# Unread products between the three pieces of the first expert's x, and narrowing steps of expert 0 shifted by one place

## The chip, the core and the metric

The kernel runs on one core of a Trainium2 chip. A core has TensorE (PE: matrix products, with PEld for its weight loads), VectorE (DVE), ScalarE (ACT), GpSimd (POOL) and SyncE (SP, which here only issues DMAs); each works through its own list of instructions in order and waits at an instruction until what that instruction reads has been written, or what it overwrites has been read. The metric is the device time of one execution in microseconds (us), as the median of several runs.

## The reference

Three layers stand one behind the other, all in float32:

```
state = alpha[t] * state + k[t] (x) v[t];  y[t] = q[t] @ state      # 4 x 8 heads, 768 steps, 48 wide
logits = x @ w_gate                                                  # x: 3072 tokens x 384
# greedy over all (token, expert) pairs by logit, each expert takes at most 384 tokens
out[mask_e] = relu(x[mask_e] @ w1[e]) @ w2[e]                        # 8 experts, 384 -> 1024 -> 384
h = out @ w_in;  result = (relu(h) ** 2) @ w_out                     # 384 -> 2048 -> 384
```

So every token goes through exactly one expert and then through a second, shared pair of matrices, w_in and w_out.

## The kernel before

**The stages.** The first 150 us are the attention (24 blocks of 128 steps). Then the experts follow one by one, and each is taken with the 384 tokens that are assigned to it: a router step finds the expert that fills first and its tokens, POOL gathers their rows of x from DRAM in three pieces of 128 tokens, PE transposes the pieces, and four chains of products follow: gemm1 (x by w1, 8 blocks f), gemm2 (by w2), gemm3 (by w_in, 16 blocks f) and gemm4 (by w_out). Each product in float32 accuracy is three products of rounded parts (high by high, low by high, high by low), so a block of gemm1, 2, 3 or 4 is nine products of 128x384. The expert that is done first is called expert 0 here, the next one expert 1.

**The first x.** For expert 0, `x_tr(0)` transposes piece after piece (j = 0, 1, 2; three transposes each) into PSUM, and `evac` copies to a rounded high part xh on ACT and the remainder xl on DVE: once for pieces 0 and 1 together, once for piece 2. Ahead of it the router writes the token numbers ix, and `warm(24)` puts 24 products on PE whose result (in acc[2]) nobody reads. `warm` is there from before at two other places too (3 and 8 products).

**The narrowing.** w_in and w_out come in as 64-bit words that hold float64 numbers, and `narrow` turns each of the 16 blocks of weights into a float32 number and splits that into a high and a low part. It is a generator with four steps for each block, which this text calls A (line 183), B (187), C (191) and D (203), all on DVE; each is two instructions of 128x384 while expert 0 runs. Between C and D, ACT must round the number to the high part (line 197, called H here, two instructions): it is put into `pend` at C and recorded at the next call of `highs()`, or at the latest in D. D subtracts the high part. H also overwrites the raw words, so it waits for C.

**Where the steps stand.** All order is the order in which the Python code records instructions, engine by engine. In gemm1 of expert 0, `highs(); next(wl[0], None); next(nw, None)` runs one narrowing step per block f, behind the splitting of one piece of the expert's own weights (lines 841 and 842). In gemm3 and gemm4 of expert 0 there are two steps per block f: one behind gemm3(f+1) and one behind gemm4(f), each behind a call of `highs()`. The steps are used up within block 12. gemm3(f) reads block f of the narrowed weights.

**What else stands on DVE there.** For each block gl (line 956), the low part of the squared activations, which the third product of gemm4 reads; two pieces of the next expert's weights (lines 813 on ACT and 814 on DVE); the router of expert 1, which runs in small steps between the products (counts on PE at line 464, votes at line 537, comparisons at line 456 on DVE), and the first part of the router of expert 2 (from line 426); and from block 12 on the evacuation of expert 1's x (`xl`, line 860), of which the next transposes (line 878) wait, since they use the same PSUM buffer xq_p.

Of the kernel before, what the change touches and what calls it, by code (L numbers as in the profile page):

```python
# [53 lines left out]
def kernel(ctx, tc, q, k, al, v, wg, w1, w2, w_in, w_out, out):  # L54
# [118 lines left out]
    def narrow():  # L173

        for f in range(NF2):
            raw = raws[f, 0]
            if fine[0] is None:
                ps = [(aw.tile([128, NWP], U32, name="nb"), slice(0, NWP))]
            else:
                ps = [(fine[0].tile([128, DM], U32, name="nb", tag="ob", bufs=3), slice(i * DM, (i + 1) * DM))  # L180
                      for i in range(2)]
            for t, cs in ps:
                nc.vector.tensor_scalar(t, raw[:, cs, 1], 3, 0x3FFFFFF8, op0=OP.logical_shift_left,
                                        op1=OP.bitwise_and)
            yield
            for t, cs in ps:
                nc.vector.scalar_tensor_tensor(t, raw[:, cs, 1], 0xC0000000, t, op0=OP.bitwise_and,
                                               op1=OP.bitwise_or)
            yield
            for t, cs in ps:  # L190
                nc.vector.scalar_tensor_tensor(t, raw[:, cs, 0], 29, t, op0=OP.logical_shift_right,  # L191
                                               op1=OP.bitwise_or)
            w = consts.tile([128, 2, NWP], FR, name=f"w{f}", tag=f"w{f}")

            def high(w=w, ps=ps):
                for t, cs in ps:
                    nc.scalar.activation(w[:, 0, cs], t.bitcast(FT), AF.Copy)

            pend.append(high)
            yield  # L200
            highs()
            for t, cs in ps:
                nc.vector.tensor_tensor(w[:, 1, cs], t.bitcast(FT), w[:, 0, cs].bitcast(FT), op=OP.subtract)  # L203
            wi[f] = w[:, :, :DM].rearrange("p h (a b) -> p h a b", a=KD)
            wo[f] = w[:, :, DM:]
            yield
# [3 lines left out]
    def highs():  # L210

        while pend:
            pend.pop()()
# [175 lines left out]
    def warm(n):  # L389

        jf = jc.rearrange("p a b -> p (a b)")
        for _ in range(n):
            nc.tensor.matmul(acc[2], jf[:, :128], jf[:, 128:128 + CAP], start=True, stop=True)
# [98 lines left out]
    def routing(kk):  # L492
# [155 lines left out]
            yield  # L648
            nc.tensor.matmul(fp, low, pr_, start=True, stop=True)
        if kk == 0:  # L650
            warm(24)
        ix = mr.tile([128, NT], I32, name="ix", bufs=2)
        for g in range(4):
            V.tensor_scalar(ix[32 * g:32 * (g + 1)], fp[:, NT * g:NT * (g + 1)], float(N // 2), None,
# [42 lines left out]
    nw = narrow()  # L697
# [149 lines left out]
    def w_upto(n):  # L847

        while wdone[0] < min(n, 24):
            next(wl[0])  # L850
            wdone[0] += 1

    def x_tr(kk):
        xh = mw.tile([128, KD, CAP], FR, name="xh", tag="tzh")
        xl = mw.tile([128, KD, CAP], FR, name="xl", tag="tzl")
        XT[kk] = (xh, xl)

        def evac(kd, xf, a=0, b=CAP):
            nc.scalar.activation(xh[:, kd, a:b], xf, AF.Copy)
            nc.vector.tensor_tensor(xl[:, kd, a:b], xf, xh[:, kd, a:b].bitcast(FT), op=OP.subtract)  # L860

        if kk == 0:
            banks = [xq_p, hu_p[0], hu_p[2]]
            banks = [[b[:, j * 128:(j + 1) * 128] for b in banks] for j in range(NT - 1)]
            banks.append([a[:, :128] for a in acc])
            for j in range(NT):
                for kd in range(KD):
                    nc.tensor.transpose(banks[j][kd], XG[kk][:, j, kd * 128:(kd + 1) * 128], ident)
                if j == NT - 2:
                    for kd, b in enumerate((xq_p, hu_p[0], hu_p[2])):  # L870
                        evac(kd, b[:, :256], 0, 256)
                elif j:
                    for kd in range(KD):
                        evac(kd, banks[j][kd], 256, CAP)
            return
        for kd in range(KD):
            for j in range(NT):
                nc.tensor.transpose(xq_p[:, j * 128:(j + 1) * 128], XG[kk][:, j, kd * 128:(kd + 1) * 128], ident)  # L878
            evac(kd, xq_p)
            yield  # L880
# [29 lines left out]
    def gemm1(kk, f):  # L910
        xh, xl = XT[kk]
        hp = hu()
        cs = slice(f % 2 * 128, (f % 2 + 1) * 128)
        for kd in range(KD):
            mm3(hp, (w1h[:, f // 2, kd, cs], w1l[:, f // 2, kd, cs]), (xh[:, kd, :], xl[:, kd, :]), kd == 0,
                kd == KD - 1)
            tick()
        hh = mw.tile([128, CAP], FR, name="hh", tag="eh")
        hl = mw.tile([128, CAP], FR, name="hl", tag="el")
        nc.scalar.activation(hh, hp, AF.Relu)  # L920
        nc.vector.scalar_tensor_tensor(hl, hp, 0.0, hh.bitcast(FT), op0=OP.max, op1=OP.subtract)  # L921
        return hh, hl

    def gemm2(f, h, ms=range(KD)):
        for m in ms:
            cs = slice(m * 128, (m + 1) * 128)
            mm3(acc[m], (w2h[:, f, cs], w2l[:, f, cs]), h, f == 0, f == NF1 - 1)
            tick()

    def z_evac():  # L930
        zh = mw.tile([128, KD, CAP], FR, name="zh", tag="tzh")
        zl = mw.tile([128, KD, CAP], FR, name="zl", tag="tzl")
        for m in range(KD):
            nc.scalar.activation(zh[:, m, :], acc[m], AF.Copy)
            nc.vector.tensor_tensor(zl[:, m, :], acc[m], zh[:, m, :].bitcast(FT), op=OP.subtract)
        return zh, zl
# [61 lines left out]
    def wstep():  # L998
        if wdelay[0] > 0:
            wdelay[0] -= 1  # L1000
        else:
            w_upto(wdone[0] + 1)
# [7 lines left out]
    for _ in x_tr(0):  # L1010
        pass
    h = gemm1(0, 0)
    rn = routing(1)
    for kk in range(E):
        more = kk + 1 < E
        rt[0] = rn if more else iter(())
        held[:] = True, False
        for f in range(NF1):
            if f == 0:
                beat[:] = (T0 if kk else 11), T1  # L1020
            if f == NF1 - 1:
                beat[0] = T2
            hn = gemm1(kk, f + 1) if f + 1 < NF1 else None
            if kk == 0:
                highs()
                next(wl[0], None)
                next(nw, None)
                if f == 0:
                    next(rn)
            w_upto(15 + 3 * (f // 2))  # L1030
            wstep()
            wstep()
            if f == NF1 - 2:
                gemm2(f, h, (0, 1))
                h6 = h
            elif f == NF1 - 1:
                gemm2(f, h, (0,))
                gemm2(f - 1, h6, (2,))
                gemm2(f, h, (1, 2))
            else:  # L1040
                gemm2(f, h)
            h = hn
        held[0] = False
        z = z_evac()
        g = gemm3(z, 0)
        beat[1] = T3
        for f in range(NF2):
            if not more and f == NF2 - 3:

                g1 = gemm3(z, f + 1)  # L1050
                g2 = gemm3(z, f + 2, True)
                for fj, gj, j in ((f, g, 0), (f + 1, g1, 0), (f, g, 1), (f + 1, g1, 1), (f + 2, g2, 0)):
                    gemm4(fj, gj, (j,))
                o_evac(kk, (0,))
                gemm4(f + 2, g2, (1,))
                o_evac(kk, (1,))
                for fj, gj in ((f, g), (f + 1, g1), (f + 2, g2)):
                    gemm4(fj, gj, (2,))
                o_evac(kk, (2,))
                return  # L1060
            if f + 1 < NF2:
                gn = gemm3(z, f + 1)
            elif more:
                for _ in rt[0]:
                    pass
                w_upto(12)
                h = gemm1(kk + 1, 0)
            if kk == 0:
                highs()
                next(nw, None)  # L1070
            if more and f == XF + 3:
                next(xt, None)
            gemm4(f, g)
            g = gn
            if kk == 0:
                highs()
                next(nw, None)
            wstep()
            if more and f == XF:
                for _ in rt[0]:  # L1080
                    pass
                xt = x_tr(kk + 1)
            if more and f > XF:
                next(xt, None)
            if kk + 2 < E and f == 11:
                rn = routing(kk + 2)
                next(rn)
            if kk + 2 < E and f == 13:
                next(rn)
        o_evac(kk)  # L1090
# [48 lines left out]
```

## Time and profile before

| what | value |
|---|---|
| runs without profile | 836.4, 837.15, 839.09 us; median 837.15 |
| the profiled execution's own time | 840.04 us, of which the span of the trace is 837.7 |
| PE busy | 778.7 us, 93% of the span |
| DVE busy | 532.7 us, 64% |
| ACT busy | 390.9 us, 47% |
| mean granted clock of PE | 0.968 of full speed |
| share of PE in the chain that ended last | 63% |

Times in the rows are microseconds from the start of the span. A granted clock of 1.00 is 2.4 GHz, 0.50 is 1.2 GHz. In a timeline the first number is the start, the second the duration, and the bracket at the end says how long the engine had been idle and what it had waited for. PE's products overlap: a stream of products of 128x384 starts one every 0.17 us at full clock although each lasts 0.33.

### The profile page before, as it was taken

Reading aid. Unit: us, or ns where it says so; the run is one execution under the profiler, and the core shown is the slowest. Engines: PE = TensorE matmul, PEld = TensorE weight load, DVE = VectorE, ACT = ScalarE, POOL = GpSimd, SP = SyncE. Lnnn points to the kernel's source line nnn. Section 1 sums busy time; section 2 is a strip of 40 time slices with the busy share of each in tenths; the row PEclk is TensorE's granted clock in tenths of the full one; section 3 lists DMA queues with packets and bytes.
Section 4 is the critical chain, followed back from the end, with each engine's and each line's share of the span. In section 5 each row is a group of like instructions: output and inputs, shape, how many; then the busy total and the mean of one; then the engine's idle time right before and its main releaser. Section 6 shows DMA issues by size and latency. Waiting matters only on the chain.

```text
span 837.7 us, 15297 instructions
## 1 busy us (share of the span) xinstructions
PE 778.7 (93%) x5830; PEld 733.1 (88%) x5830; DVE 532.7 (64%) x1454; ACT 390.9 (47%) x934; POOL 126.0 (15%) x146
## 2 busy tenths in 40 slices
PE   3888887788998899999999999999999999999996
PEld 2766666568997899999999999999999999999996
DVE  7999998757788665676567656665765543442211
ACT  2656655222455424643463456245524643661443
POOL 3222210020001211122112211221211110101001
PEclk9989999579999899999999999999999999999999
DMA  8998886150022100320131023004200330310000
GB/s 303 236 264 259 256 255 246 67 180 1 1 76 85 49 1 29 114 67 2 57 110 42 1 76 103 30 1 123 86 1 24 119 109 15 89 35 29 1 1 28
DMA packets 32440, 74.77 MB, mean 89 GB/s; under 512 B 4128, under 2 KB 14112, under 8 KB 32368
## 3 DMA queue, kind: packets, MB, share of 16 engines
q1 hardware_dynamic: 25840, 59.65, 23.7%
q0 software_dynamic: 3072, 9.44, 3.3%
q10 hardware_dynamic: 3456, 4.72, 1.6%
q8 instruction: 45, 0.74, 0.4%
q14 instruction: 27, 0.22, 0.1%
HBM read 64.36 MB, written 9.44 MB: 88 GB/s over the span
## 4 chain that ended last, share of the span: by engine, by line
PE 63%; issue 9%; DVE 6%; ACT 2%; POOL 1%; DMA 1%; SPq 0%; ACTq 0%; POOLq 0%; DVEq 0%
PE hu_p L885 10%; PE hu_p L887 10%; PE hu_p L886 10%; PE acc L969 7%; PE acc L965 6%; PE acc L970 6%; PE acc L885 3%; PE acc L887 3%; PE acc L886 3%; PE rt_p L464 1%; DVE nb L191 1%; PE xq_p L878 1%; PE rt_p L472 1%; POOL out_dram L991 1%; DVE w L203 1%
## 5 line engine op out<-in xcount | busy, mean ns | idle before, releaser
L956 DVE TENSOR_TENSOR gl<-rg,gh 128x384 fp32r<-128x384 f32 x127 | 72.0, 567 | 159.1 <-ACT rg L955 158.3
L953 ACT ACTIVATE rg<-hu_p 128x384 f32<-128x384 f32 x128 | 62.9, 491 | 157.6 <-PE hu_p L887 156.6
L885 PE MATMUL hu_p<-zh,w 128*128 128x384 f32 x384 | 132.9, 346 | 0.0
L969 PE MATMUL acc<-w,gh 128*128 128x384 f32 x381 | 130.6, 343 | 0.0
L887 PE MATMUL hu_p<-zl,w 128*128 128x384 f32 x384 | 130.1, 339 | 0.0
L886 PE MATMUL hu_p<-zh,w 128*128 128x384 f32 x384 | 130.1, 339 | 0.0
L965 PE MATMUL acc<-w,gl 128*128 128x384 f32 x381 | 126.4, 339 | 3.2 <-DVE gl L956 3.2
L970 PE MATMUL acc<-w,gh 128*128 128x384 f32 x381 | 128.0, 336 | 0.0
L920 ACT ACTIVATE hh<-hu_p 128x384 fp32r<-128x384 f32 x64 | 31.5, 492 | 148.8 <-PE hu_p L887 136.7
L921 DVE SCALAR_TENSOR_TENSOR hl<-hu_p,hh 128x384 fp32r<-128x384 f32 x64 | 35.6, 556 | 69.7 <-ACT hh L920 69.7
L484 POOL PARTITION_ALL_REDUCE tot<-ex x40 | 43.1, 1079 | 227.9 <-DVE ex L481 227.9
L965 PEld LDWEIGHTS acc<-w,gl 128*128 128x128 f32 x381 | 71.6, 189 | 4.5 <-DVE gl L956 4.4
L887 PEld LDWEIGHTS hu_p<-zl,w 128*128 128x128 f32 x384 | 72.4, 189 | 1.0
L885 PEld LDWEIGHTS hu_p<-zh,w 128*128 128x128 f32 x384 | 72.5, 189 | 0.1
L886 PEld LDWEIGHTS hu_p<-zh,w 128*128 128x128 f32 x384 | 72.6, 189 | 0.0
L969 PEld LDWEIGHTS acc<-w,gh 128*128 128x128 f32 x381 | 71.9, 189 | 0.6 <-ACT gh L954 0.4
L970 PEld LDWEIGHTS acc<-w,gh 128*128 128x128 f32 x381 | 71.9, 189 | 0.0
L954 ACT ACTIVATE gh<-rg 128x384 fp32r<-128x384 f32 x127 | 66.7, 525 | 4.0
L885 PE MATMUL hu_p<-xh,w1h 128*128 128x384 f32 x192 | 67.0, 349 | 0.0
L887 PE MATMUL hu_p<-xl,w1h 128*128 128x384 f32 x192 | 65.9, 343 | 0.0
L885 PE MATMUL acc<-hh,w2h 128*128 128x384 f32 x192 | 65.7, 342 | 0.0
L886 PE MATMUL hu_p<-xh,w1l 128*128 128x384 f32 x192 | 65.5, 341 | 0.0
(238 smaller groups left out, 1500.0 us busy)
## 6 DMA issues: line engine op xcount, KB each, us to landing
wraw<-in_w_dram SPq DMA_DIRECT2D x62, 384.0 KB, 3.2
raw<-in_w_in_dram SPq DMA_DIRECT2D x16, 384.0 KB, 6.3
raw<-in_w_out_dram SPq DMA_DIRECT2D x16, 384.0 KB, 7.9
vt<-in_v_dram SPq DMA_DIRECT2D x12, 384.0 KB, 6.9
x_d<-xo ACTq DMA_DIRECT2D x24, 192.0 KB, 4.6
a<-in_al_dram SPq DMA_DIRECT2D x9, 451.9 KB, 6.6
k<-in_k_dram SPq DMA_DIRECT2D x9, 448.0 KB, 6.2
q<-in_q_dram SPq DMA_DIRECT2D x9, 448.0 KB, 5.4
```

The costliest lines, as they stand in the source:

```text
L484: nc.gpsimd.partition_all_reduce(tot[:, :, :J], ex[:, :, :J], 128, bass_isa.ReduceOp.add)
L885: nc.tensor.matmul(dst, wh, xh, start=first, stop=False)
L886: nc.tensor.matmul(dst, wl, xh, start=False, stop=False)
L887: nc.tensor.matmul(dst, wh, xl, start=False, stop=last)
L920: nc.scalar.activation(hh, hp, AF.Relu)
L921: nc.vector.scalar_tensor_tensor(hl, hp, 0.0, hh.bitcast(FT), op0=OP.max, op1=OP.subtract)
L953: nc.scalar.activation(r, up, AF.Relu)
L954: nc.scalar.activation(gh, r, AF.Square)
L956: nc.vector.tensor_tensor(gl, g, gh.bitcast(FT), op=OP.subtract)
L965: nc.tensor.matmul(acc[j], gl[:, j * 128:(j + 1) * 128], wo[f][:, 0, :], start=False, stop=(f == NF2 - 1))
L969: nc.tensor.matmul(acc[j], gh[:, cs], wo[f][:, 0, :], start=(f == 0), stop=False)
L970: nc.tensor.matmul(acc[j], gh[:, cs], wo[f][:, 1, :], start=False, stop=False)
```

## The change

Three edits. In the router of expert 0, 29 unread products stand where 24 stood. In `x_tr(0)`, five unread products stand behind the transposes of piece 0 and three behind those of piece 1. And in gemm1 of expert 0, block f = 3 runs a second narrowing step, so that from there on every narrowing step of expert 0 stands one place earlier.

```
@@ routing, expert 0
-            warm(24)
+            warm(29)
@@ x_tr(0)
             for j in range(NT):
                 for kd in range(KD):
                     nc.tensor.transpose(banks[j][kd], XG[kk][:, j, kd * 128:(kd + 1) * 128], ident)
+                warm((5, 3, 0)[j])
                 if j == NT - 2:
@@ gemm1 of expert 0
                 next(nw, None)
                 if f == 0:
                     next(rn)
+                if f == 3:
+                    next(nw, None)
```

PE, between the transposes of piece 1 and those of piece 2 (xg is the gathered x, jc a table of constants); the rows with + are new.

```order
 L868 MATMUL xq_p<-ident,xg 128x128
 L868 MATMUL hu_p_2098<-ident,xg 128x128
 L868 MATMUL hu_p_2100<-ident,xg 128x128
+L393 LDWEIGHTS jc
+L393 MATMUL acc_2103<-jc 128x384
+L393 LDWEIGHTS jc
+L393 MATMUL acc_2103<-jc 128x384
+L393 LDWEIGHTS jc
+L393 MATMUL acc_2103<-jc 128x384
 L868 MATMUL acc_2101<-ident,xg 128x128
 L868 MATMUL acc_2102<-ident,xg 128x128
 L868 MATMUL acc_2103<-ident,xg 128x128
```

Three products more stand ahead of the transposes of the last piece; behind piece 0 five stand in the same way.

DVE, in gemm3 and gemm4 of expert 0, blocks 10 and 11 (gl as above; 814 splits the next expert's weights; 191 is C, 203 D, 183 A, 187 B). Before:

```order
L956 TENSOR_TENSOR gl<-rg,gh 128x384
L814 TENSOR_TENSOR w1l<-wraw,w1h 128x256
L191 SCALAR_TENSOR_TENSOR nb<-raw_1818,nb 128x384 x2
L203 TENSOR_TENSOR w_3191<-nb,w_3191 128x384 x2
L814 TENSOR_TENSOR w1l<-wraw,w1h 128x256
L956 TENSOR_TENSOR gl<-rg,gh 128x384
L814 TENSOR_TENSOR w2l<-wraw,w2h 128x256
L183 TENSOR_SCALAR nb<-raw_1821 128x384 x2
L187 SCALAR_TENSOR_TENSOR nb<-raw_1821,nb 128x384 x2
L814 TENSOR_TENSOR w2l<-wraw,w2h 128x256
```

The same two blocks after (gl is line 957 there):

```order
L957 TENSOR_TENSOR gl<-rg,gh 128x384
L814 TENSOR_TENSOR w1l<-wraw,w1h 128x256
L203 TENSOR_TENSOR w_3182<-nb,w_3182 128x384 x2
L183 TENSOR_SCALAR nb<-raw_1821 128x384 x2
L814 TENSOR_TENSOR w1l<-wraw,w1h 128x256
L957 TENSOR_TENSOR gl<-rg,gh 128x384
L814 TENSOR_TENSOR w2l<-wraw,w2h 128x256
L187 SCALAR_TENSOR_TENSOR nb<-raw_1821,nb 128x384 x2
L191 SCALAR_TENSOR_TENSOR nb<-raw_1821,nb 128x384 x2
L814 TENSOR_TENSOR w2l<-wraw,w2h 128x256
```

C and D stood side by side behind one gl; now B and C stand behind one, D and A behind the next. ACT's list has H at the same place as before, behind gl's own inputs.

DVE, ahead of the first evacuation of expert 1's x (line 860), before:

```order
L956 TENSOR_TENSOR gl<-rg,gh 128x384
L814 TENSOR_TENSOR w2l<-wraw,w2h 128x256
L191 SCALAR_TENSOR_TENSOR nb<-raw_1821,nb 128x384 x2
L203 TENSOR_TENSOR w_3285<-nb,w_3285 128x384 x2
L814 TENSOR_TENSOR w2l<-wraw,w2h 128x256
L860 TENSOR_TENSOR xl<-xq_p,xh 128x384
```

The same place after:

```order
L957 TENSOR_TENSOR gl<-rg,gh 128x384
L814 TENSOR_TENSOR w2l<-wraw,w2h 128x256
L203 TENSOR_TENSOR w_3257<-nb,w_3257 128x384 x2
L814 TENSOR_TENSOR w2l<-wraw,w2h 128x256
L860 TENSOR_TENSOR xl<-xq_p,xh 128x384
```

C of the last block has left this place; it stands ahead of the router of expert 2 now.

## Rows read from the trace of the kernel before

**Rows 1.** Timeline of PE, 170 to 200 us: start, duration, instruction, [idle before].

```profile
172.22 4.07 PE L393 MATMUL acc<-jc 128*128 128x384 f16 x24
177.46 0.30 PE L868 MATMUL xq_p<-ident,xg 128*128 128x128 f32 x1 [1.17 <-ACT w1h L841]
...
179.40 0.33 PE L868 MATMUL xq_p<-ident,xg 128*128 128x128 f32 x1 [1.42 <-DMA xg<-x_d,ix]
...
180.88 0.90 PE L868 MATMUL acc<-ident,xg 128*128 128x128 f32 x3 [0.93 <-DMA xg<-x_d,ix]
181.72 0.69 PE L885 MATMUL hu_p<-xh,w1h 128*128 128x384 f32 x1
...
187.38 0.34 PE L885 MATMUL acc<-hh,w2h 128*128 128x384 f32 x1
...
193.56 1.60 PE L464 MATMUL rt_p<-m,oh 128*8 128x63 f16 x24 [1.85 <-DVE m L456]
```

**Rows 2.** Windows, PE alone: stretch, length, PE busy, granted clock, DMA share, GB/s.

```profile
180.00:180.50 0.50, 0.00 (x0) 0.73 0.44 172
...
187.00:187.50 0.50, 0.50 (x4) 0.94 0.22 86
```

**Rows 3.** Windows, all engines (PE, PEld, DVE, ACT, POOL busy, then granted clock).

```profile
400.00:600.00 200.00, 200.00 (x1187) 196.05 (x1186) 127.21 (x445) 99.11 (x233) 36.03 (x41) 1.00 0.21 63
...
275.00:276.00 1.00, 0.00 (x0) 0.00 (x0) 1.00 (x4) 1.00 (x4) 0.00 (x0) 0.90 0.71 286
...
282.50:283.00 0.50, 0.50 (x4) 0.50 (x3) 0.50 (x2) 0.50 (x2) 0.00 (x0) 0.87 0.00 0
```

**Rows 4.** Timeline of PE, waits of expert 0's gemm4 and of expert 1's transposes.

```profile
253.86 0.44 PE L965 MATMUL acc<-w,gl 128*128 128x384 f32 x1 [1.34 <-DVE gl L956]
260.97 0.45 PE L965 MATMUL acc<-w,gl 128*128 128x384 f32 x1 [0.40 <-DVE gl L956]
...
272.85 0.45 PE L965 MATMUL acc<-w,gl 128*128 128x384 f32 x1 [1.05 <-DVE gl L956]
276.55 0.90 PE L878 MATMUL xq_p<-ident,xg 128*128 128x128 f32 x3 [2.21 <-DVE xl L860]
```

**Rows 5.** Timeline of DVE, steps C, D, then gl and A; and xl.

```profile
256.67 1.02 DVE L191 SCALAR_TENSOR_TENSOR nb<-raw,nb 128x384 uint32<-128x384 uint32 x2
258.29 1.03 DVE L203 TENSOR_TENSOR w<-nb,w 128x384 fp32r<-128x384 f32 x2 [0.59 <-ACT w L197]
...
260.35 0.56 DVE L956 TENSOR_TENSOR gl<-rg,gh 128x384 fp32r<-128x384 f32 x1 [0.70 <-ACT rg L955]
...
261.17 0.62 DVE L183 TENSOR_SCALAR nb<-raw 128x384 uint32<-128x384 uint32 x2
...
275.94 0.55 DVE L860 TENSOR_TENSOR xl<-xq_p,xh 128x384 fp32r<-128x384 f32 x1
```

**Rows 6.** Timeline of ACT: step H (L197) ahead of D at 258.29.

```profile
257.73 0.94 ACT L197 ACTIVATE w<-nb 128x384 fp32r<-128x384 f32 x2 [3.53 <-DVE nb L191]
```

**Rows 7.** Timeline of ACT: the weight piece rg is rounded.

```profile
187.97 0.84 ACT L841 ACTIVATE w2h<-rg 128x768 fp32r<-128x768 f32 x1
```

**Rows 8.** Timeline of SP: the issue of two pieces rg.

```profile
179.79 0.86 SPq L828 DMA_DIRECT2D rg<-in_w_dram  x2
```

**Rows 9.** Tile rg, 178 to 215 us: time from issue to landing.

```profile
DMA to landing us min/median/max: 3.9/3.9/3.9
```

**Rows 10.** Timeline of PE in the attention, and its clock by windows.

```profile
79.12 1.16 PE L240 MATMUL sc_p<-q,k 48*128 48x128 f32 x16 [1.36 <-issue]
80.22 0.60 PE L249 MATMUL kt_p<-ident,k 112*128 112x112 f32 x4
```

**Rows 11.** Windows, PE alone, over that place: granted clock behind the busy time.

```profile
77.83:81.24 3.41, 2.12 (x28) 1.00 1.05 281
```

**Rows 12.** Timeline of DVE: a comparison of the router of expert 1.

```profile
207.71 0.55 DVE L456 TENSOR_TENSOR m<-xn,jc 128x744 f16<-128x744 f16 x1
```

**Rows 13.** Timeline of PE: the count that reads it.

```profile
209.95 0.91 PE L464 MATMUL rt_p<-m,oh 128*8 128x31 f16 x24
```

More of the change, by code (lines that the diff above doesn't have):

```diff
@@ L650, in routing @@
         if kk == 0:
-            warm(24)
+            warm(29)
         ix = mr.tile([128, NT], I32, name="ix", bufs=2)
@@ L868, in x_tr @@
                     nc.tensor.transpose(banks[j][kd], XG[kk][:, j, kd * 128:(kd + 1) * 128], ident)
+                warm((5, 3, 0)[j])
                 if j == NT - 2:
@@ L1029 @@
                     next(rn)
+                if f == 3:
+                    next(nw, None)
             w_upto(15 + 3 * (f // 2))
```

## The prediction

> **What bounds the kernel now.** I read the share of busy time first: PE is the busiest engine, and a look by windows shows it busy all the time from 400 to 600 us [rows 3], so what is won well before that reaches the end unshortened. Then I looked for what PE loses between 170 and 290 us, where the change lies, in three views: the windows with the granted clock, the timeline of PE with its waits, and the timelines of DVE and ACT behind those waits.
>
> Two things show. First, the clock. It falls from full to half at about 180.2 and is full again at about 187.0 [rows 2], a slow stretch of 6.8 us; it falls again at about 275.8 and rises at 282.6 [rows 3], 6.8 us too. Ahead of the first fall PE ran out of dense products at 172.22 + 4.07 = 176.29 and then had only six transposes, with gaps of 1.17 and 1.42 us, until 179.94 or so [rows 1]. Ahead of the second stand the waits of 1.05 and 2.21 us [rows 4]. The slow stretch costs: 18 products start between 181.72 and 187.38, one every 0.314 us; the 24 unread products of the same 384 columns, at full clock, came one every 4.07 / 24 = 0.17 [rows 1].
>
> Second, the waits of PE on DVE [rows 4]: 1.34, 0.40, 1.05 and 2.21 us, with a second one of the kind of the 0.40 one block pair later (0.39), in all 5.4 us. Behind the 0.40 us stands a blocked ACT, not a busy DVE. H waits 3.53 us for C [rows 6]; ReLU and squares of the next block stand behind H in ACT's list, so they come late, and DVE then sits idle for 0.70 us before gl [rows 5]. The same neighbourhood costs DVE 0.59 us between C and D, in which D waits for H.
>
> **Part 1, the five added products ahead of piece 0.** They last 5 x 0.17 = 0.85 us and end at 177.14 instead of 176.29. Piece 0 is transposed at 177.46, when its rows have landed [rows 1]. Cost nothing; the gather covers them, with 0.3 us to spare.
>
> **Part 2, the products between the pieces.** The three transposes of a piece take some 0.5 us at full clock (an estimate: the third piece needs 0.90 at half clock, its first one latency included). Piece 0 ends at 177.96, five products at 178.81; piece 1 comes at 179.40. It ends at 179.9, three products at 180.43; piece 2 comes at 180.88 [rows 1]. So the cover is 0.6 and 0.45 us, and the path does not get longer. At half clock the products would take 5 x 0.314 = 1.6 and 3 x 0.314 = 0.95 us and end 0.2 and at most 0.1 us too late: that is the upper bound of the cost, 0.3 us.
>
> What they may bring is the clock. Of the 4.6 us from 176.3 to 180.9 PE was busy for about 1.0; it will be for about 3.3, and no gap is longer than 0.6 us. The nearest rows: a single gap of 1.34 us in dense products ahead of 253.86 left the clock full (the product behind it lasted 0.44 us [rows 4], the one at 181.72 at half clock 0.69), and so did a gap of 1.36 us at 77.8 in the attention, behind which there were only 16 short products and then transposes [rows 10, 11]. From these I take it that the clock stays full. Then the 18 products save 18 x (0.314 - 0.17) = 2.6 us and the third piece's transposes about 0.1 of path: 2.7 us. Bounds: 0.3 lost, 2.7 won.
>
> Does that pass on? PE's next wait is the 1.85 us at 193.56 on a comparison of expert 1's router [rows 1]. DVE's work ahead of it runs without a break from the splitting of piece rg, and this starts on ACT at 187.97 [rows 7], right behind the second ReLU, so it comes with PE. Only the landing could hold it: issued at 179.79 [rows 8], 3.9 us later [rows 9] there, at 183.7, while it is now wanted at 185.3. So everything moves by 2.7 us; the wait of 1.85 us stays.
>
> The Trainium skill, page "TensorE: Matmul & The Clock Gate", section "Part 4: PE-mode transpose", says that the full clock does not engage for transposes, which do not count as PE being busy in the same way. The row at 77.83 speaks rather against it, since there the clock stayed 1.00 over a stretch that held four transposes (0.60 us [rows 10]) and a few more; by the rule the sum would lack these 2.7 us (first rival).
>
> **Part 3, the narrowing steps.** No step is added; at f = 3 of gemm1 C comes ahead of its turn, and then each place has the step that stood one place later. In gemm1 itself I cost this at nothing. At that place C (1.02 us) stands ahead of a comparison of expert 1's router that ended at 207.71 + 0.55 = 208.26 [rows 12], and PE wants it at 209.95 [rows 13], so 1.69 us are spare and 0.7 are left. If that cover were gone PE would wait up to 1.0 us.
>
> In gemm3 and gemm4 the gain lies, wait by wait:
> - 260.97 and its like: C is now done in the block before, beside B, so H finds it done and no longer blocks ACT. ReLU follows PE, gl is in time. 0.40 + 0.39 = 0.8 won.
> - 276.55: xl (275.94 [rows 5]) had C, the wait of 0.59 and D right ahead; now only D. C goes with 0.95 (start to start, its two halves overlap a little) and the wait with 0.59: 1.5 won, 0.7 stay.
> - 253.86: gl stood behind C, wait, D and a burst of the router; now behind D, A and the burst. C + 0.59 + D = 2.5 becomes D + A = 0.95 + 0.55 = 1.5 [rows 5]: 1.0 won. But the other half pair becomes B + C = 1.9 in place of A + B = 1.5, and a small product of the router between these blocks, for which DVE has the input ready only just in the timeline, will wait these 0.4 us. Net 0.6.
> - 272.85: gl behind the first part of expert 2's router, with B + C ahead where A + B stood: 0.4 lost, but gl of the block before comes 0.70 + 0.3 earlier relative to PE. 0.6 won.
> - Each wait that is gone also spares the longer first product behind it (0.44 against 0.33 [rows 1, 4]), 0.1 x 3 = 0.3.
>
> Sum 0.8 + 1.5 + 0.6 + 0.6 + 0.3 = 3.8 us. DVE's work is otherwise the same, so it cannot be less than nothing by itself; the upper bound is all the waits, 5.4.
>
> With waits of at most 0.7 us in place of 1.05 and 2.21 the second fall should not come either. PE worked from 276.55 to 282.6 at half clock: 6.05 x (1 - 0.17 / 0.314) = 2.8 us won. Bounds 0 and 2.8.
>
> **Sum.** 2.7 + 3.8 + 2.8 = 9.3 us off the profiled execution's 840.04 (span 837.7 and 2.3 around it, which the change doesn't touch) gives 830.7. The runs shown have a median of 837.15, 2.9 us below it. Part of that may be slow stretches that cover fewer products there, in which case it can't be won twice: between none and all of 2.9, I take half, 1.45. So 9.3 - 1.45 = 7.85 us off 837.15: 829.3 us.
>
> **Rivals.**
> 1. The clock falls at the first x as before, since transposes do not hold it. For it: the fall at 180.2 came with six transposes in the stretch. Against: the attention row [rows 11]. The 2.7 us stay lost, the narrowing's 3.8 + 2.8 = 6.6 remain, less 1.1 for the median: 831.7 us. Chance 0.15.
> 2. DVE as a whole is the bound between 240 and 277, and waits only move: gl in time at 260, later elsewhere, and the clock still falls at 275.8. For it: DVE is nearly always busy there, and its work does not shrink. Against: 0.59 and 0.70 us of idle DVE for each block pair [rows 5], which the new order takes away. Only the first x is won: 2.7 less 0.7: 835.2 us. Chance 0.12.
> 3. Both: no change that can be seen, 837.2. Chance 0.06.
> 4. Slower. DVE is the bound from gemm1 on, and C at f = 3 is paid by the router of expert 1, whose chain count, vote, comparison alternates between PE and DVE in six rounds. If the comparison comes more than 1.69 us later than at 208.26, each of the four rounds left makes PE wait up to 1.0 us, 4 in all, and a slow stretch (2.8) may follow. The second stretch's gains are eaten too, since DVE is late there as well. 4.0 + 2.8 less the 2.7 of the first x: 837.15 + 4.1 = 841.2 us. Against: 0.7 us of cover are left, and ends of DVE there have idle in front. Chance 0.05.
>
> **Numbers.** The forecast has 0.62, with a range of its own from 826 to 832.5. The range from 825.5 to 834.8 takes in rival 1 and part of rival 2, about 0.8 in all; its low end is the sum with all waits gone (5.4 in place of 3.8) and nothing taken off for the median, 2.7 + 5.4 + 2.8 = 10.9, so 826.2, and a little for what the rows do not show. What a measurement of this kernel can tell from no change is about 0.3%, 2.5 us. Faster than 834.6: forecast, rival 1 and a share of 2, 0.80. Within: most of 2, and 3, 0.15. Slower: 0.05.
>
> **What would show it.** Right: granted clock 1.00 from 170 to 190 us; the nine products of gemm1's first block at 0.17 us; acc of the first gemm2 product at about 184.7 in place of 187.38; H without an idle of over 1 us ahead of it that ends with C; D without its 0.59; no wait of the 260.97 kind, xl's wait at 0.7; clock 1.00 through the transposes of expert 1's x. Wrong: a fall between 178 and 184 (rival 1); waits on gl that add up to 3 us or more between 240 and 280 (rival 2); waits at the counts between 203 and 235 that were not there (rival 4).

## The result, and the profile after

The changed kernel takes 830.29 us (median of five runs, 828.0 to 832.24); the kernel before, run beside it, 837.37 us. The ratio is 0.9915 (95% interval 0.9901 to 0.9929), so 7.1 us are won (5.9 to 8.3). The forecast was 829.3, in a range from 825.5 to 834.8. The profiled execution's own time was 832.24 us (span 830.4, mean granted clock 0.969).

Timeline of PE after, at the same place as [rows 1]:

```profile
174.81 6.50 PE L393 MATMUL acc<-jc 128*128 128x384 f16 x29
181.14 0.27 PE L868 MATMUL xq_p<-ident,xg 128*128 128x128 f32 x1
...
181.47 0.98 PE L393 MATMUL acc<-jc 128*128 128x384 f16 x5
182.28 0.27 PE L868 MATMUL xq_p<-ident,xg 128*128 128x128 f32 x1
...
182.61 0.65 PE L393 MATMUL acc<-jc 128*128 128x384 f16 x3
183.10 0.49 PE L868 MATMUL acc<-ident,xg 128*128 128x128 f32 x3
183.75 0.44 PE L886 MATMUL hu_p<-xh,w1h 128*128 128x384 f32 x1 [0.16 <-ACT xh L859]
...
187.23 0.33 PE L886 MATMUL acc<-hh,w2h 128*128 128x384 f32 x1
193.41 1.60 PE L464 MATMUL rt_p<-m,oh 128*8 128x63 f16 x24 [1.85 <-DVE m L456]
195.22 0.52 PE L887 MATMUL acc<-hh,w2l 128*128 128x384 f32 x1
195.54 0.52 PE L888 MATMUL acc<-hl,w2h 128*128 128x384 f32 x1
```

Windows of PE alone, after: granted clock at the two places of [rows 2], behind the count, and where the second fall stood in [rows 3].

```profile
180.00:180.50 0.50, 0.50 (x6) 1.00 0.42 74
187.00:187.50 0.50, 0.50 (x5) 1.00 1.03 399
195.50:198.50 3.00, 3.00 (x11) 0.50 0.00 0
275.00:276.00 1.00, 1.00 (x7) 1.00 0.03 8
```

Both slow stretches that the prediction spoke of are gone: from the first gemm1 product at 183.75 to gemm2 at 187.23 the clock is full, and so it is at expert 1's x. Three things are not as forecast. The 29 products take 6.50 us, not 29 x 0.17, as the clock came back to full only at about 178 (before: 170); the first transposes start right behind them, with no gap left. Behind the count's wait of 1.85 us, which is as long as before, the products last 0.52: the half clock there is the same as before. And everything stands 2.2 us later than before from the last vote of expert 0's router on, before any changed instruction.

Timeline of PE before, behind the same count:

```profile
195.58 0.52 PE L886 MATMUL acc<-hh,w2l 128*128 128x384 f32 x1
195.90 0.52 PE L887 MATMUL acc<-hl,w2h 128*128 128x384 f32 x1
```

Waits of PE in gemm3 and gemm4 of expert 0 and at expert 1's x, after (timeline of PE; they answer to [rows 4]):

```profile
248.02 0.17 PE L649 MATMUL rt_p<-pr__3022,low 128*32 128x12 f16 x1 [0.36 <-DVE pr__3022 L647]
...
253.18 0.45 PE L966 MATMUL acc<-w,gl 128*128 128x384 f32 x1 [0.27 <-DVE gl L957]
...
269.86 0.45 PE L966 MATMUL acc<-w,gl 128*128 128x384 f32 x1 [0.37 <-DVE gl L957]
271.94 0.55 PE L879 MATMUL xq_p<-ident,xg 128*128 128x128 f32 x3 [0.59 <-DVE xl L860]
```

Timeline of DVE after, two blocks (the place of [rows 5]):

```profile
256.39 1.02 DVE L203 TENSOR_TENSOR w<-nb,w 128x384 fp32r<-128x384 f32 x2
257.33 0.62 DVE L183 TENSOR_SCALAR nb<-raw 128x384 uint32<-128x384 uint32 x2
...
259.01 1.02 DVE L187 SCALAR_TENSOR_TENSOR nb<-raw,nb 128x384 uint32<-128x384 uint32 x2
259.94 1.02 DVE L191 SCALAR_TENSOR_TENSOR nb<-raw,nb 128x384 uint32<-128x384 uint32 x2
...
261.22 0.56 DVE L957 TENSOR_TENSOR gl<-rg,gh 128x384 fp32r<-128x384 f32 x1
```

Timeline of ACT after, step H (the place of [rows 6]):

```profile
255.37 0.94 ACT L197 ACTIVATE w<-nb 128x384 fp32r<-128x384 f32 x2 [0.99 <-DVE nb L187]
...
261.11 0.92 ACT L197 ACTIVATE w<-nb 128x384 fp32r<-128x384 f32 x2
```

The four waits are 1.59 us together, where before had 5.69 (the 5.4 of the prediction and 0.30 on a small product of the router). D no longer waits for H, gl starts without idle, and H waits 0.99 us or nothing where it had waited 3.53. The row of the 0.99 names B, but C stands right behind B and ended at 255.33: H still starts with the end of C, only that it comes early enough for ReLU behind it.

### The profile page after: what moved, and what is told of

It reads as the page before. It is cut to its first block, busy times and chain, and to the rows that moved or that the text cites. A ratio compares the mean times of both kernels' runs of the same rounds, so it can differ in the third digit from the quotient of the medians.

```text
span 830.4 us, 15330 instructions
## 1 busy us (share of the span) xinstructions
PE 780.5 (94%) x5843; PEld 734.1 (88%) x5843; DVE 532.5 (64%) x1454; ACT 390.7 (47%) x934; POOL 125.3 (15%) x146
## 4 chain that ended last, share of the span: by engine, by line
PE 66%; issue 9%; DVE 5%; ACT 1%; POOL 1%; DMA 0%; ACTq 0%; POOLq 0%; DVEq 0%
PE hu_p L886 11%; PE hu_p L888 10%; PE hu_p L887 10%; PE acc L970 7%; PE acc L966 7%; PE acc L971 6%; PE acc L886 3%; PE acc L888 3%; PE acc L887 3%; PE acc L393 1%; PE rt_p L464 1%; PE xq_p L879 1%; PE rt_p L472 1%; POOL out_dram L992 1%; DVE w L203 1%
## 5 line engine op out<-in xcount | busy, mean ns | idle before, releaser
L956 ACT ACTIVATE rg<-rg 128x384 f32<-128x384 f32 x128 | 65.1, 509 | 0.0
```

Source lines behind the costliest of these rows:

```text
L956: nc.scalar.activation(g, r, AF.Square)
```

## The experiments

**How they are read.** Single executions differ by 2 us for reasons outside the change: the last vote behind the attention, whose code is untouched, stands between 166.87 and 169.22 us, with slow stretches of the clock at other places each time. So each profile is cut at four instructions, and a part is compared with the same part. *Gather* runs from the last vote of expert 0's router (DVE) to the end of POOL's third gather of x; *x* from there to the first product of gemm2; *count* from the first count of expert 1's router to the first product of gemm3; *narrowing* from there to expert 1's first gemm1 product. Between x and count lie 6.17 or 6.18 us in all of them, and behind the last cut 554.25 to 554.47.

| kernel (profile) | gather | x | count | narrowing | median us | ratio to before |
|---|---|---|---|---|---|---|
| before, 1st | 11.80 | 8.59 | 25.99 | 63.83 | 837.4 | 1 |
| before, 2nd | 11.45 | 7.36 | 26.27 | 62.61 | | |
| before, 3rd | 11.36 | 7.27 | 26.28 | 62.62 | | |
| the change, 1st | 11.68 | 6.33 | 26.54 | 56.05 | 830.29 | 0.9915 [0.9901, 0.9929] |
| the change, 2nd | 12.30 | 6.02 | 26.56 | 56.03 | | |
| x alone | 11.68 | 6.43 | 26.54 | 62.60 | 836.87 | 1.0001 [0.9989, 1.0012] |
| narrowing alone | 11.68 | 7.51 | 24.98 | 56.00 | 830.7 | 0.9924 [0.9911, 0.9938] |
| shift by two | 11.68 | 6.38 | 26.94 | 60.38 | 834.45 | 0.9963 [0.9949, 0.9976] |
| change + ten at the count | 11.68 | 6.39 | 24.99 | 56.03 | 828.73 | 0.9892 [0.9877, 0.9907] |
| narrowing + ten | 11.49 | 7.38 | 24.99 | 56.03 | 830.38 | 0.9905 [0.9888, 0.9922] |
| 24, 5, 3 + ten | 11.32 | 5.96 | 24.99 | 56.04 | 828.34 | 0.9882 [0.9865, 0.9899] |
| 24, 5, 3 | 11.68 | 6.00 | 26.28 | 56.01 | 829.77 | 0.9899 [0.9880, 0.9918] |
| 29 ahead only | 11.32 | 7.29 | 26.32 | 56.03 | 830.73 | 0.9913 [0.9894, 0.9932] |
| transposes in place | 11.68 | 6.49 | 26.55 | 56.03 | 830.06 (one run) | |

The median of before was 837.3 to 838.3 us, by the chip; each ratio is against the runs on its own chip.

**1. The products at the first x alone.** The change without its last edit:

```
-            warm(24)
+            warm(29)
...
+                warm((5, 3, 0)[j])
```

> The 29, 5 and 3 unread products alone, without the narrowing step at f = 3. Theory (the two parts are independent): the clock stays full through the transposes of the first x, and from the last vote of expert 0's router to the first product of the first gemm2 it takes about 18.0 us instead of 20.4, as in the changed kernel; the waits of 240 to 280 us and the slow stretch there are as before (5.7 us of waits). Time 837.4 - 2.4 = about 835.0 us. Rival (the narrowing does it all): no difference from before, 837 us. Rival (the products free the later stretch too): under 833 us.

Measured: 836.87 us, ratio 1.0001. The expected gain did not come. The profile has no slow stretch at the x (x part 6.43), as the theory has it, though its clock came back late (9); the time hardly shows it, and is the number of the first rival. The waits of 240 to 280 us are 5.69 us and the slow stretch is there, as before. The parts say where the gain went: against the second and third profile of before (7) the x part is 0.8 to 0.9 us shorter, but gather is 0.2 to 0.3 and count 0.3 longer, and from the last vote to gemm3 it takes 50.83 us where those took 51.25 and 51.09. That is 0.3 to 0.4 us, less than the interval of the ratio can show.

**2. The narrowing alone.** The other half:

```
+                if f == 3:
+                    next(nw, None)
```

> The narrowing step at f = 3 alone; 24 products ahead of the first x and none between its pieces. Theory: the clock falls at the first x as before; between the first gemm3 product and the first product of expert 1's gemm1 it takes about 56 us instead of 63.8, with waits of 1.2 us instead of 5.7. Time 837.4 - 5 to 7 = 830.5 to 832.5 us, by the profiles 7.8 us below before. Rival (the x products do more than their own 2.4 us): above 834 us.

Measured: 830.7 us, ratio 0.9924, as expected. The 6.4 us that it wins are nine tenths of the change's 7.1, and its waits of the same four kinds are those of the change (1.58 us). Its profile has the slow stretch at the x (7.51) but, alone among the eleven profiles without added products there, none behind the count (24.98).

**3. Shifted by two places.** If what counts is that the steps are early, two are as good as one:

```
                 if f == 3:
                     next(nw, None)
+                    next(nw, None)
```

> The changed kernel with two added narrowing steps at f = 3 instead of one, so that all steps stand two places earlier and C and D stand behind the same gl again. Theory (what counts is which steps share a block): H blocks ACT again, D waits about 0.59 us for it again, waits of PE on gl come back (some 4 to 6 us in all between 240 and 275); only the wait on xl is gone, and the fall of the clock at 275 perhaps with it. Time 833 to 836 us, 3 to 6 us slower than the changed kernel. Rival (what counts is that the steps come earlier): as fast as the changed kernel or faster, 828 to 830.5 us.

Measured: 834.45 us, ratio 0.9963, as the theory has it; more than half of the narrowing's gain is lost again. The place of the steps in the block decides: with two, C and D stand side by side behind one gl again. (A count of expert 1's router, at 209.15, also waits 0.33 us for its comparison here, which it does in neither before nor after.) Timelines of ACT, DVE and PE of this kernel:

```profile
255.00 0.94 ACT L197 ACTIVATE w<-nb 128x384 fp32r<-128x384 f32 x2 [3.63 <-DVE nb L191]
```

```profile
255.56 1.03 DVE L203 TENSOR_TENSOR w<-nb,w 128x384 fp32r<-128x384 f32 x2 [0.59 <-ACT w L197]
...
257.62 0.56 DVE L957 TENSOR_TENSOR gl<-rg,gh 128x384 fp32r<-128x384 f32 x1 [0.70 <-ACT rg L956]
```

```profile
258.24 0.45 PE L966 MATMUL acc<-w,gl 128*128 128x384 f32 x1 [0.39 <-DVE gl L957]
...
273.82 0.45 PE L966 MATMUL acc<-w,gl 128*128 128x384 f32 x1 [1.61 <-DVE gl L957]
```

These are the numbers of before to 0.1 us [rows 4 to 6]: H's 3.53, D's 0.59, gl's 0.70, PE's 0.40. That chain, H blocked behind C, ReLU behind H, gl behind ReLU, is shown by it. The clock stayed full at expert 1's x here, so the other 4.3 us of the narrowing part (60.38 against 56.05) are waits alone, 5.15 us in place of 1.59, and the slower starts behind them.

**4. Ten unread products ahead of the count.** If the half clock behind the 1.85 us wait is what takes time, PE must not stand still there (`warm` has a second argument here, the tile that it writes):

```
+                    if kk == 1 and i == 0:
+                        warm(10, xq_p)
                     for a, b in parts:
                         key.count(i, a, b)
```

> The changed kernel, and ten more unread products ahead of the first count of expert 1's router, into the PSUM bank that the transposes used, where PE waits 1.85 us for a comparison on DVE and the clock falls behind it. Theory (clock): the ten products fit the wait (10 x 0.17 = 1.7 us), the clock stays full behind it, where 9 to 12 products run at half clock in the profiles, and 1.3 to 1.8 us are won in executions that had the fall there: 828.5 to 829.5 us. Rival: the fall there is not due to the wait, or the products come late to something: 830.3 us or above.

Measured: 828.73 us, ratio 0.9892, as expected. Timeline of PE of this kernel:

```profile
189.53 1.80 PE L393 MATMUL xq_p<-jc 128*128 128x384 f16 x10
191.53 1.60 PE L464 MATMUL rt_p<-m,oh 128*8 128x63 f16 x24 [0.21 <-DVE m L456]
193.06 0.44 PE L888 MATMUL acc<-hh,w2h 128*128 128x384 f32 x1
193.35 0.34 PE L889 MATMUL acc<-hh,w2l 128*128 128x384 f32 x1
```

The wait is filled but not shortened: the count still comes 6.17 us behind gemm2's first product. Won is the clock behind it (0.34 where after has 0.52): the count part 24.99 instead of 26.54.

**5. The same ten without the products at the x.** From the runs so far I had a theory: what the products at the x win is given back at the count, where the clock then falls instead. Narrowing alone was its witness. So: the narrowing's edit and experiment 4's, with `warm(24)` and nothing between the pieces.

> The shifted narrowing and ten unread products ahead of the first count of expert 1's router, without the products at the first x. Theory 'given back': with the narrowing alone the clock did not fall behind the wait at that count (count to first product of gemm3 24.98 us, not 26.54), so there is nothing for the ten products to win: 830.7 us as without them (830.0 to 831.3), and the products at the first x are worth the 2 us by which the kernel with both stands lower (828.73). Rival 'each by itself': the ten products are worth 1.5 to 2 us whatever stands at the first x, and those at the first x nothing: 828.5 to 829.3. The profile is to show the count's wait at 0.2 instead of 1.85 us in either case; dp (last vote of expert 0) to the first product of gemm2 is to stay near 19.2 to 20.4 us.

Measured: 830.38 us, ratio 0.9905. The median is where "given back" puts it. But by the ratio, which leaves the chip out, the ten are worth 1.6 us here (0.9924 to 0.9905) and 1.9 beside the x products (0.9915 to 0.9892), and each ratio is good to some 1.3 us either way: this run can't tell. The profiles of before do (7).

**6. 24 products ahead, not 29.** In experiment 4's kernel:

```
-            warm(29)
+            warm(24)
```

> The changed kernel with ten unread products ahead of the first count of expert 1's router, and 24 instead of 29 products ahead of the first piece of x (5 and 3 between the pieces stay). Theory: in the profile of the changed kernel the 29 products began at half clock and ended some 1.1 us after the first piece's rows were there; without five of them the first transposes come up to 0.8 us earlier, of which the next gather, not PE, sets the rest, so the first product of gemm2 comes 0 to 0.3 us earlier: 828.4 to 828.8 us. Rival: the five products are what brings the clock to full before the gather; without them it stays or falls to half in the pieces and the 2 us are lost: 830 to 831.5.

Measured: 828.34 us, ratio 0.9882, the lowest of all. The five products more are not needed in this profile: without them there is no slow stretch at the pieces, and the x part is 5.96 in place of 6.39. The clock was full from 169.8 on here and from 176.3 in experiment 4's profile, so the 0.43 us are not those of the five products alone; for the same reason gemm2 comes 0.8 us earlier behind the last vote, not 0 to 0.3. Against experiment 5, on the same chip, it differs only by the 5 and 3 products: 2.0 us less by the medians (827.6 to 828.8 against 829.0 to 831.6), 1.4 by the x part.

**7. Before, twice more.** The kernel before, unaltered.

> The kernel before once more, unaltered. Theory 'the loss at the first x differs from one execution to the next': the slow stretch at the first x covers fewer products than in the first profile, so last vote to first product of gemm2 is 18.5 to 19.5 us instead of 20.39, and the execution is that much faster than 840.04. Rival 'a fixed loss': 20.39 again within 0.2. In either case the clock falls at the transposes of expert 1's x (gemm3's first product to expert 1's gemm1 62 to 64 us).

> The kernel before a third time, unaltered. Theory 'the slow stretch at the first x differs from one execution to the next, and the first profile had a long one': last vote to first product of gemm2 18.5 to 19.5 us (18.81 in the second profile, 20.39 in the first). Rival 'long and short come equally often': 20.2 to 20.6 us again. At the transposes of expert 1's x the clock falls in either case, gemm3's first product to expert 1's gemm1 62 to 64 us.

Measured: 837.93 and 837.01 us. Timeline of PE, third profile of before:

```profile
181.33 0.69 PE L885 MATMUL hu_p<-xh,w1h 128*128 128x384 f32 x1
...
183.42 0.52 PE L885 MATMUL hu_p<-xh,w1h 128*128 128x384 f32 x1
183.74 0.41 PE L886 MATMUL hu_p<-xh,w1l 128*128 128x384 f32 x1
183.99 0.33 PE L887 MATMUL hu_p<-xl,w1h 128*128 128x384 f32 x1
```

Only seven or eight products run at half clock, where the first profile had 18: the slow stretch lasts 3.4 us (180.5 to 183.9), not 6.8. The x part is 7.36 and 7.27, not 8.59, and the narrowing part 62.61 and 62.62, not 63.83: at expert 1's x, too, the first profile had the long stretch and the others a short one. Both show the half clock behind the count as well (26.27, 26.28). So it falls there whether it fell at the x or not, and "given back" is wrong: ten of the eleven profiles without the ten products have that fall, narrowing alone is the exception, and none of the three with them has it.

**8. 24, 5 and 3, and 29 ahead without anything between.** Each is the changed kernel with one of its two edits at the x undone. For 24, 5, 3 it is the first pair of lines, for the 29 alone the last line:

```
-            warm(29)
+            warm(24)
...
-                warm((5, 3, 0)[j])
```

> The changed kernel with 24 instead of 29 products ahead of the first piece of x; 5 and 3 between the pieces and the shifted narrowing stay. Theory 'the 5 and 3 hold the clock, the five ahead only cost': last vote to first product of gemm2 17.3 us (as with the ten products at the count added) and not 18.0, no slow stretch at the pieces, 829.3 to 829.8 us. Rival 'the 29 are needed, or the count gives the gain back': 830.3 or more. The wait at the first count (1.85 us) stays, with a slow stretch of 3.4 us behind it in most executions.

> The changed kernel without the 5 and 3 products between the pieces; the 29 ahead and the shifted narrowing stay. Theory 'the 5 and 3 hold the clock': the clock falls at the pieces or right behind them as without any (179 to 188 us), last vote to first product of gemm2 18.8 to 19.5 us, 830.7 to 831.5 us. Rival 'the 29 alone hold it' : no slow stretch between the pieces and the first product of gemm2, 17.8 to 18.1 us, 829.5 to 830.3 us.

Measured on one chip: 829.77 us for 24, 5, 3 and 830.73 for the 29 alone. Timeline and windows of PE with the 29 alone:

```profile
172.32 4.89 PE L393 MATMUL acc<-jc 128*128 128x384 f16 x29
178.15 0.30 PE L868 MATMUL xq_p<-ident,xg 128*128 128x128 f32 x1 [0.94 <-issue]
...
180.47 0.90 PE L868 MATMUL acc<-ident,xg 128*128 128x128 f32 x3 [0.64 <-DMA xg<-x_d,ix]
```

```profile
181.50:182.00 0.50, 0.50 (x2) 0.50 1.02 350
182.50:183.00 0.50, 0.50 (x3) 0.50 1.30 412
```

And with 24, 5, 3, timeline of PE:

```profile
172.89 4.07 PE L393 MATMUL acc<-jc 128*128 128x384 f16 x24
178.17 0.30 PE L868 MATMUL xq_p<-ident,xg 128*128 128x128 f32 x1 [1.21 <-issue]
...
181.02 0.55 PE L868 MATMUL acc<-ident,xg 128*128 128x128 f32 x3
...
182.35 0.34 PE L886 MATMUL hu_p<-xh,w1h 128*128 128x384 f32 x1
```

With full clock from the start and gaps of 0.94 and 0.64 us the 29 alone do not hold the clock; the 5 and 3 do, even behind a gap of 1.21. The x part is 7.29 against 6.00. From the last vote to gemm2 it is 18.6 against 17.7 us, each a little off its forecast (18.8 to 19.5, and 17.3). So what the x part wins comes from the products between the pieces. When the clock had come back is no rival here: it was full 3.0 and 3.1 us behind the last vote in the first profile of before and with the 29 alone, which have the slow stretch, and 3.0 with 24, 5, 3 and the ten, which has none; 4.5 us behind it with the narrowing alone, which has it, and 4.3 with 24, 5, 3, which has none. The x part is 1.4 to 1.5 us shorter with the 5 and 3 in 24, 5, 3 + ten against narrowing + ten, and in 24, 5, 3 against narrowing alone.

**9. Transposes in their place.**

```
-                warm((5, 3, 0)[j])
+                for _ in range((8, 5, 0)[j]):
+                    nc.tensor.transpose(acc[2][:, :128], ident, ident)
```

> The changed kernel with unread transposes (8 and 5, of the identity, 128x128 float32) between the pieces of x instead of the 5 and 3 unread products. If transposes hold the clock as products do: granted clock 1.00 from the rise on to the first product of gemm2, and last vote to that product 18.0 to 18.3 us. If they don't: a fall at the pieces (179 to 187 us) and 19.2 to 20.4 us.

Measured, windows of PE over the last piece and gemm1:

```profile
181.50:182.00 0.50, 0.36 (x2) 1.00 1.17 385
183.00:183.50 0.50, 0.50 (x4) 1.00 1.25 234
```

The clock is full through the pieces and gemm1, the x part 6.49, the whole from the last vote 18.17 us, all as with products. This is one profile, and one in which the clock had come back at 176 only, so the 29 products ran up to the pieces; that transposes could hold it behind a gap is not shown, and no kernel with so late a clock ran without anything between the pieces.

**10. The changed kernel once more.**

> The changed kernel once more, unaltered. Theory 'the 29 products come late because the clock is back to full at 176 to 179 us only, as in the five profiles with 29': the 29 take 6.4 to 6.6 us again and last vote to first product of gemm2 is 18.0 to 18.2 us. Rival 'when the clock comes back differs from one execution to the next': back at 170 to 172 us as in the five profiles with 24, the 29 take some 5 us and the stretch is 17.3 to 17.5 us.

Measured: 832.20 us; clock full from about 178, the 29 products 6.56 us long, 18.32 us to gemm2. That was the first theory's number, apart from a third gather that took 0.6 us longer on POOL.

## Why the prediction was right, and where not

The direction, the size of the whole and the two mechanisms were right; the terms were not, and two errors cancelled: the slow stretches were priced too high (2.7 and 2.8 us, where 0.8 to 1.2 and 1.6 were measured), the waits too low (3.8, where 4.1 and 0.9 behind them were measured), and what was taken off for the median covered most of the rest. That the forecast came within 1 us is in part luck.

**Part 1 (cost nothing, 0.3 us of cover).** Wrong where the clock was late. When it is back only at 176 to 178 us, the 29 products take 6.5 us in place of 4.9 and there is no cover. After shows it: the first gather ended at 177.86, and with 24, 5, 3 the first transposes come 2.2 us behind that (175.93 to 178.17), so they could have come at 180.1; they came at 181.14. The third piece loses only 0.1 to 0.2 of it, the rest is in xh and xl of pieces 0 and 1, which come late (0.16 in the row at 183.75). The x part is 6.33 to 6.49 us in five of the six profiles with 29 products and a late clock, 5.96 and 6.00 with 24: the price is 0.4 us, for 29 products and a late clock against 24 and an early one. No profile has 24 with a late clock, so the two are not taken apart.

**Part 2 (2.7 us).** The mechanism is right: no slow stretch in any profile with products between the pieces, one in each without. Of the former only the two with 24 ahead can be set beside one without at a like clock (8); the others had the late clock. The price is the step that failed: "18 x (0.314 - 0.17)" took the 18 products of one profiled execution. In two others of the same kernel it was seven or eight, 8 x 0.144 = 1.2 us, and the x part tells the same: from 7.27 to 7.51 without the products to 6.33 to 6.49, 0.8 to 1.2 us with the 0.4 of part 1 in it. The kernel with x alone shows even less, none within its interval of 1 us, and the change against the narrowing alone no difference clear of noise (0.9915 against 0.9924). So the time that the three edits at the x win in this change is not shown; that the 5 and 3 alone win time is, beside 24 ahead (6). The comparison of gaps left out the nearest row against it: the 1.85 us at 193.56 [rows 1] are a single gap in dense products too, and behind them the products of before last 0.52 us. That what is won there passes on almost whole was right: x to count is 6.17 us everywhere, the wait of 1.85 stays, and the count part of before is 26.0 to 26.3 against 26.5, so at most 0.5 us is lost behind it.

**Part 3 (3.8 + 2.8 = 6.6 us).** Measured 62.61 - 56.05 = 6.6 us against the second and third profile, with other terms. The mechanism held but for one step: H does not find C long done, it starts 0.04 us behind C's end after 0.99 us of waiting in one block, and without a wait in the next, and that is early enough for ReLU and gl. The waits gave 5.69 - 1.59 = 4.1 where 3.5 stood (0.8, 1.5, 0.6 and 0.6): those of the 260.97 kind went (0.8, as forecast), xl's 2.21 became 0.59 (1.6 for 1.5), 1.05 became 0.37 (0.7 for 0.6), 1.34 became 0.27 (1.1), and the small router product pays 0.36, as forecast, while another's 0.30 is gone. The second fall gave not 2.8 but 1.6: from gemm3's first product behind the transposes to gemm1 it is 5.12 us in before's third profile (275.68 to 280.80) and 3.57 after (272.43 to 276.00), since the stretch there is the short one (rows below). 0.9 is left for the starts behind waits, where I had 0.3; about 0.3 us a wait fits, but no run takes it apart.

Timeline of PE, third profile of before, gemm3's first product behind the transposes and gemm1's first:

```profile
275.68 0.42 PE L885 MATMUL hu_p<-zh,w 128*128 128x384 f32 x1
...
280.80 0.34 PE L885 MATMUL hu_p<-xh,w1h 128*128 128x384 f32 x1
```

The same two after:

```profile
272.43 0.42 PE L886 MATMUL hu_p<-zh,w 128*128 128x384 f32 x1
...
276.00 0.34 PE L886 MATMUL hu_p<-xh,w1h 128*128 128x384 f32 x1
```

**The median.** I took half of the 2.9 us between the profiled execution and the median off, for slow stretches that are shorter elsewhere. The second and third profile say it was nearly all: 1.2 us in the x part and 1.2 in the narrowing part. With all of it off, the same sum gives 837.15 - (9.3 - 2.9) = 830.75; measured 830.29.

**The rivals.** Rival 1 (the clock falls at the x anyway) did not come. Behind it stood the rule of the Trainium skill ("TensorE: Matmul & The Clock Gate", section "Part 4: PE-mode transpose") that transposes don't engage the full clock. The nearest test is experiment 9, where only transposes stood between the pieces, and there the trace differs: 1.00 at 181.5 to 183.5 us behind eight and five of them, though with dense products until right ahead of the first piece. Rival 2 fell with the waits (1.59, not 3). Rival 4's waits did not come: the count that reads the comparison with C ahead of it started at 210.35 without idle (0.91 us long, as in [rows 13]).

**What stays open.** Why the clock came back at 170 to 172 us in eight profiles and at 176 to 178 in six, though the code ahead is the same. All six have 29 products ahead and something between the pieces; I know no reason for that and no run takes chance out. The profiles do show that the two kinds part ahead of any changed instruction: at the end of the attention the clock fell 21.6 to 21.8 us before the last vote in the six, and 20.5 to 20.9 or 22.9 to 23.0 us before it in the eight. So the 29 products themselves, which run behind the last vote, did not make the clock late.

## What to carry to other kernels

A slow stretch of the clock in one profile is one draw: price it by two or three profiles of the same kernel, stage by stage, before it becomes a term. When a step on one engine waits for a conversion on another, move it so that its input is done when its turn comes, and check where its neighbours land: one place won 6.4 us here, two places (with the products at the x) 3. Unread products belong where PE stands still ahead of dense work (5 and 3 between gathers, ten ahead of a count: 828.34 us with 24, 5, 3), and their number should be one that ends before what they wait beside, also when the clock is late.

## What the hardware showed unexpectedly

At half clock gemm products of 128x384 start one every 0.32 us, at full clock every 0.175. Slow stretches of the same place in the same kernel were 6.8 us in one execution and 3.4 in two others. A wait of 1.85 us on PE in dense work was followed by half clock in ten of eleven executions, soon after PE started again; the same wait with ten products in it and 0.21 us of idle in none of three.
